# Long convolution beside a feed-forward block: the second transforms of the convolution as 64x32 tiles in plain float32 after a butterfly, with one four-bank buffer

## The chip, the core and the metric

The kernel runs on one core of a Trainium2 chip. The metric is the device time of one execution in microseconds (us), lower is better. TensorE (PE in the profile) does the matrix products, VectorE (DVE) and ScalarE (ACT) the elementwise work, GpSimd (POOL) and SyncE (SP) issue most of the transfers. Matrix products land in PSUM, eight banks of 128 partitions by 512 float32 numbers; everything else on the chip lives in SBUF.

## The reference

The input is `x` (2048 positions, 576 channels). It is normalized, and the output is the sum of the input and two branches:

```python
xn = layernorm(x)
return x + A(xn) + B(xn)
# A: K[d, l] = Re sum_n C[d,n] * exp(dt[d] * A[d,n] * l) * dt[d] * B[d,n], l = 0..2047
#    y = irfft(rfft(xn padded to 4096) * rfft(K padded to 4096))[:2048] + xn * Dskip
# B: silu(xn @ w1) @ w2, w1 is 576 x 4608, w2 is 4608 x 576
```

Branch B is the bulk of the arithmetic. Branch A is a causal convolution along the positions, one filter of 2048 taps per channel.

## The kernel before, in words

**Number format.** The large products are in the format that the code calls F32R. A float32 operand is split into a rounded high part and a remainder, and a product is made of three matrix products (high by high, high by low, low by high) that add up in PSUM. The small products of the tile form 64x32 or 128x32 are in plain float32; the profile shows two records for each of them.

**The feed-forward part** (`ffn`, `up` and `down`) works in blocks: half of the positions, 4 tiles of 128 hidden features, a group of 512 positions. `up` makes one 128x512 tile of the hidden layer (lines L331 to L333), which ACT passes through SiLU and rounds (`gf`, `gh`, L339 and L340) and DVE splits (`gl`, L342). `down` makes one 128x288 half of an output tile with 12 products (L357, PSUM tile `po`), and DVE adds it to the sum in SBUF (`acc`, L361).

**The convolution** is a transform of length 2048 in two steps. Positions are split in 32 by 64 and frequencies likewise. The first step, over 32 positions, is done for the input by `spread` (L161, L162, result in `d1u` in DRAM) and for the filter by `kgen` (which builds the filter in tables; products `kp` at L696 and `z` at L711; result in `d1k`, stored by L724). Then `Dskip` is added to the first rows of `d1k` by a transfer that accumulates (L727).

**The second step** is `spectral`, the place of the change. For each of 32 outer frequencies k it loads 128 rows of `d1u` and of `d1k` (real and imaginary part of 64 positions) on the SP queue, splits both in high and low (`split_of`, L812 on ACT and L813 on DVE), and multiplies each with the 128x128 matrix of that frequency, three products for each half of the channels (`mm3`, L826; PSUM tiles `pk` for the filter, `pu` for the input). ACT copies the spectrum of the filter out in four pieces (`ka`, `kb`, L750 to L753), DVE multiplies the two spectra (L756 to L759) out of PSUM, the product is split, and a second matrix takes it back (`pb`, L826, three products for each half). ACT copies that out (`yo`, L778), and POOL stores it in `d2` (L779). Later `conv_load` and `add_conv` do the last step over 32 frequencies as 16 products in 64x32 tiles of plain float32 (`py`, L847), eight times in the last 80 us.

**PSUM.** `ps1` has two banks (`ph`), `ps2` three (`po`), `pss` three (everything of the convolution).

**The order of the work.** The convolution is a side stream. `weave` advances it between the steps of the feed-forward part: each `yield` of the side stream names the share of the steps at which it goes on. `marks` in `side` gives the shares at which the filter's tables begin, the second step begins and ends: 0.13, 0.597 and 0.823; `tail_at` those of the last step. A scheduler then makes a fixed order for each engine, by priorities (`high_priority`) and by `issue_after` (called through `behind`), which keeps an instruction behind a named one of the same engine. Each engine and each queue executes its order strictly one after the other.

Of the kernel before, what the change touches and what calls it, by code (L numbers as in the profile page):

```python
# [43 lines left out]
def kernel(  # L44
# [15 lines left out]
    cf1: bass.AP,  # L60
    cm23: bass.AP,
    cs4: bass.AP,
    cv: bass.AP,
    out: bass.AP,
):
# [22 lines left out]

    cst = ctx.enter_context(tc.tile_pool(name="cst", bufs=1))
    ident = cst.tile([P, P], F32, name="ident")  # L90
    f1 = cst.tile([P, P], F32, name="f1")
    s4 = None
    vt = cst.tile([P, 69], F32, name="vt")
# [18 lines left out]
    acc = {}  # L112

    def new_xt(blk):
        xh = xtp.tile([P, NKT, 512], F32R, tag="xh", name=f"xh_{blk}")
# [141 lines left out]
    def ffn():  # L257
# [63 lines left out]
        def up(blk, t, a=0, e=512, after=None):  # L321

            half, c, b = blk
            xh, xl, x4 = xts[2 * half + b]
            h1, l1 = W1[half, c, t]
            pool, tag = (ps2, "ps2") if e == 256 and t > 1 else (ps1, "ps1")
            ph = pool.tile([P, 512], F32, tag=tag, name="ph")[:, a:e]
            for n, (w, v) in enumerate(((h1, xh), (h1, xl), (l1, xh))):
                for kt in range(NKT):
                    with behind(after):  # L330
                        nc.tensor.matmul(ph, w[:, kt, :], v[:, kt, a:e], start=n + kt == 0, stop=False)  # L331
            nc.tensor.matmul(ph, h1[:, 4, :], x4[:, a:e], start=False, stop=False)  # L332
            pins["pe"] = nc.tensor.matmul(ph, l1[:, 4, :], x4[:, a:e], start=False, stop=True).ins  # L333
            gf = gp.tile([P, 512], F32, tag="gf", name="gf", bufs=2)[:, a:e]
            if a == 0:
                G[blk, t] = [gp.tile([P, 512], F32R, tag=n, name=n) for n in ("gh", "gl")]
            gh, gl = (g[:, a:e] for g in G[blk, t])
            with tc.high_priority():
                nc.scalar.activation(gf, ph, AF.Silu)  # L339
                pins["gh"] = nc.scalar.copy(gh, gf).ins  # L340
                with behind(pins["w1l2"] if e == 256 else None):
                    pins["gl"] = nc.vector.tensor_sub(gl, gf, gh).ins  # L342

        def down(blk, jj):
# [5 lines left out]
                    add_conv(j, (acc[j], acc[j + 1]))  # L350
            for h in range(2):
                hs = slice(h * HD, (h + 1) * HD)
                po = ps2.tile([P, 512], F32, tag="ps2", name="po")
                n = 0
                for t in range(FT):
                    for g, w in ((0, 0), (0, 1), (1, 0)):
# [227 lines left out]
    def kgen():  # L584
        fT, phiT = kf["f"], kf["phi"]
        with tc.tile_pool(name="kg", bufs=1) as kg:
# [59 lines left out]
            for i in range(NCK):  # L646
# [72 lines left out]
                    nc.scalar.copy(sv[:, h], z[h].rearrange("p (e k c) -> p e k c", e=4, c=2))  # L719
                if r == NRUN - 2:  # L720
                    d0 = (i // NRUN) * NRUN * CH
                    kv = d1k.rearrange("(k n) (g d) -> g n k d", n=64, g=2)
                    for gp_ in range(2):
                        nc.sync.dma_start(kv[gp_, :, :, d0:d0 + NRUN * CH], stage[gp_ * 64:(gp_ + 1) * 64])  # L724
                yield (i + 1) / NCK

        nc.gpsimd.dma_start(d1k.rearrange("(k n) d -> n k d", n=P)[0],  # L727
                            dskip.unsqueeze(0).broadcast_to([32, D]), accum_op=ALU.add)

    def spectral():  # L730
        def operands(k):
            rows = slice(k * P, (k + 1) * P)
            return load_part(d1u[rows, :], "u"), load_part(d1k[rows, :], "k")

        def front(k):
            if k % 2 == 0:
                mm = kl.tile([P, 2, 4, P], F32R, tag="mm", name="mm")
                nc.gpsimd.dma_start(mm, cm23[:, k:k + 2])
                mats.append(mm)
            mk = mats[-1][:, k % 2]  # L740
            us, ks = ops.pop(k) if k in ops else (split_of(t, n) for t, n in zip(operands(k), "uk"))
            ka = kl.tile([P, D], F32, tag="ka", name="ka")
            kb = kl.tile([P, D], F32, tag="kb", name="kb", bufs=1)
            y = kl.tile([P, D], F32, tag="y", name="y", bufs=1)
            y2 = kl.tile([P, D], F32, tag="y2", name="y2", bufs=1)
            for h in range(2):
                hs = slice(h * HD, (h + 1) * HD)
                pk = pss.tile([P, 512], F32, tag="pss", name="pk")
                mm3(pk[:, :HD], [(mk[:, 0], mk[:, 1], ks)], hs)
                nc.scalar.copy(ka[:64, hs], pk[:64, :HD])  # L750
                nc.scalar.copy(ka[64:, hs], pk[:64, :HD])
                nc.scalar.mul(kb[:64, hs], pk[64:, :HD], -1.0)
                nc.scalar.copy(kb[64:, hs], pk[64:, :HD])  # L753
                pu = pss.tile([P, 512], F32, tag="pss", name="pu2")
                mm3(pu[:, :HD], [(mk[:, 0], mk[:, 1], us)], hs)
                nc.vector.tensor_mul(y[:, hs], pu[:, :HD], ka[:, hs])  # L756
                nc.vector.tensor_mul(y2[:64, hs], pu[64:, :HD], kb[:64, hs])
                nc.vector.tensor_mul(y2[64:, hs], pu[:64, :HD], kb[64:, hs])
            nc.vector.tensor_add(y, y, y2)  # L759
            return mk, split_of(y, "y")  # L760

        mats = []
        first = operands(0)
        yield 1.1
        with behind(pins["gh"]):
            ops = {0: [split_of(t, n) for t, n in zip(first, "uk")]}
        yield 1.12
        nxt = front(0)
        for k in range(32):
            mk, ys = nxt  # L770
            if k < 31:
                nxt = front(k + 1)
            yo = kl.tile([P, D], F32, tag="yo", name="yo")
            for h in range(2):
                hs = slice(h * HD, (h + 1) * HD)
                pb = pss.tile([P, 512], F32, tag="pss", name="pb")
                mm3(pb[:, :HD], [(mk[:, 2], mk[:, 3], ys)], hs)
                nc.scalar.copy(yo[:, hs], pb[:, :HD])  # L778
            nc.gpsimd.dma_start(d2.rearrange("(p k) d -> k p d", k=32)[k], yo)  # L779
            yield 1 + (k + 1) / 32  # L780


    order = iter((0, 1, 2, 3, 8, 9, 10, 11, 4, 5, 6, 7, 12, 13, 14, 15))
# [22 lines left out]

    yss = {}

    def split_of(t, tag):
        h = kl.tile([P, D], F32R, tag=tag + "h", name=tag + "h")  # L810
        l = kl.tile([P, D], F32R, tag=tag + "l", name=tag + "l")
        nc.scalar.copy(h, t)  # L812
        nc.vector.tensor_sub(l, t, h)  # L813
        return h, l

    def load_part(rows, tag):
        t = kl.tile([P, D], F32, tag=tag + "r", name=tag + "r")
        nc.sync.dma_start(t, rows)
        return t

    def mm3(dst, terms, hs):

        n = 0
# [13 lines left out]

    def add_conv(j, dsts):

        py = [pool.tile([P, 512], F32, tag=t, name="py") for pool, t in ((pss, "pss"),) * 3 + ((ps2, "ps2"),)]  # L840
# [20 lines left out]
        return (FT + i * 2 * FT + 1) / (2 * NCH * 2 * 2 * FT)  # L861

    def side():
        nonlocal s4, kl, yp, pa, tail_at
        marks = (0.13, 0.597, 0.823)
        tail_at = (0.91, 0.934, 0.967, 0.0072)
        with tc.tile_pool(name="kf", bufs=1) as kfp:
            for n in ("f", "phi"):
                kf[n] = kfp.tile([P, D], F32, name=n + "T")
            with tc.tile_pool(name="par", bufs=1) as par:  # L870
                with tc.tile_pool(name="pa", bufs=4) as pa:

# [54 lines left out]
        s4 = s4p.tile([P, 32], F32, name="s4")  # L927
        nc.gpsimd.dma_start(s4, cs4)

        with tc.tile_pool(name="kl", bufs=2) as kl:  # L930
            for at in spectral():
                yield marks[1] + (at - 1) * (marks[2] - marks[1])
        yp = ctx.enter_context(tc.tile_pool(name="yp", bufs=3))
        yield from tail()

    sd = side()
# [20 lines left out]
def _constants():  # L957
# [5 lines left out]
    s1 = np.zeros((2, 2, 32, 32, 2, 2), f8)  # L963
    f1 = np.zeros((2, 2, 32, 32, 2, 2), f8)
    for q in range(2):
        s1[:, q, :, :, :, q] = cs
# [8 lines left out]
    m2 = np.zeros((32, 2, 64, 2, 64), f8)  # L975
    m2[:, 0, :, 0, :] = c
    m2[:, 1, :, 0, :] = -s
    m2[:, 0, :, 1, :] = s
    m2[:, 1, :, 1, :] = c
# [6 lines left out]
    m3 = m3.reshape(32, P, 4, 16, 2).transpose(0, 1, 3, 2, 4)  # L986
    m23 = np.stack([m2.reshape(32, P, P), m3.reshape(32, P, P)], 1).transpose(2, 0, 1, 3)
    m23 = np.stack([*_hi_lo(m23[:, :, 0]), *_hi_lo(m23[:, :, 1])], 2)
    v = np.concatenate([-64 * np.arange(32.0) - 32, np.arange(33.0), [256, 64, 8, 1]])
    v = np.broadcast_to(v, (P, 69))  # L990
    r = {
# [2 lines left out]
        "cf1": f1,  # L994
        "cm23": m23,
        "cs4": s4,
        "cv": v,
    }
    return {k: np.ascontiguousarray(a, dtype=np.float32) for k, a in r.items()}
# [23 lines left out]
```

## Time and profile before

| What | Before |
| --- | --- |
| time, median of 3 runs | 1110.47 us (1110.06 to 1110.9) |
| span of the profiled execution, first to last instruction | 1108.2 us |
| PE busy | 1102.2 us (99% of the span) |
| DVE busy | 916.6 us (83%) |
| ACT busy | 706.9 us (64%) |
| POOL busy | 72.1 us (7%) |
| transfers, over the span | 148.56 MB, 134 GB/s |

The page gives a span for the profiled execution, and no other time of it. The timed runs are 2.3 us longer than that span, which is what lies around the first and the last instruction. Busy time counts an engine as busy while any of its instructions is under way. Products on PE overlap, so a 128x288 product has a duration of 295 ns while the next one starts 132 ns after it; the distance between two starts is the time that counts. The chain that ended last goes back from the last instruction to what released it, and tells which engine's work set the time.

### The profile page before, as it was taken

What the parts mean: (1) busy time and instruction counts of PE and PEld (TensorE: products, weight loads), DVE (VectorE), ACT (ScalarE), POOL (GpSimd) and SP (SyncE); (2) the same over time, 40 slices, a digit from 0 to 9 for tenths busy, and PEclk for the clock granted to TensorE, in tenths of its full rate; (3) what the DMA queues carried; (4) which work ended last, traced back from release to release, by engine and by line L of the source; (5) the groups of instructions that cost most, each with busy time, mean ns of one, the idle gap of its engine ahead of it and who ended that gap; (6) DMA issues with size and microseconds to landing.
All of it is one profiled execution on the core that took longest, in us unless ns stands there. A gap on an engine that the chain in (4) does not pass through costs nothing.

```text
span 1108.2 us, 22917 instructions
## 1 busy us (share of the span) xinstructions
PE 1102.2 (99%) x9167; PEld 997.5 (90%) x9167; DVE 916.6 (83%) x1543; ACT 706.9 (64%) x1222; POOL 72.1 (7%) x129
## 2 busy tenths in 40 slices
PE   9999999999999999999999999999999999999998
PEld 7989998899998899899999989999999999999887
DVE  7799899999999999999999737787778778784433
ACT  4564466676677676677867536877777878774210
POOL 1100000000000000011000000000000000000111
PEclk9999999999999999999999999999999999999999
DMA  9745512525252525264744173554544455434983
GB/s 270 190 123 160 152 50 61 120 73 131 77 121 83 116 72 118 77 174 154 206 122 103 45 179 109 162 167 123 156 145 152 138 149 170 129 107 127 241 224 87
DMA packets 175755, 148.56 MB, mean 134 GB/s; under 512 B 111088, under 2 KB 142592, under 8 KB 175520
## 3 DMA queue, kind: packets, MB, share of 16 engines
q1 hardware_dynamic: 165328, 112.63, 38.7%
q0 software_dynamic: 9568, 33.62, 9.6%
q8 instruction: 72, 1.18, 0.5%
q10 hardware_dynamic: 752, 0.85, 0.3%
q14 instruction: 35, 0.29, 0.1%
HBM read 102.53 MB, written 44.61 MB: 133 GB/s over the span
## 4 chain that ended last, share of the span: by engine, by line
PE 98%; DMA 1%; DVE 1%; SPq 0%; issue 0%; DVEq 0%
PE po L357 42%; PE ph L331 35%; PE kp L696 3%; PE ph L332 3%; PE ph L333 3%; PE pu L826 2%; PE pb L826 2%; PE pk L826 2%; PE z L711 2%; PE pu L161 1%; PE py L847 1%; DMA acc<-in_A_u_dram 1%; PE pu L162 1%; PE pt L124 0%; DVE w1l L295 0%; PE ptk L490 0%
## 5 line engine op out<-in xcount | busy, mean ns | idle before, releaser
L357 PE MATMUL po<-w2l,gh 128*128 128x288 f32 x1152 | 338.5, 295 | 0.0
L357 PE MATMUL po<-w2h,gl 128*128 128x288 f32 x1152 | 336.4, 295 | 0.0
L357 PE MATMUL po<-w2h,gh 128*128 128x288 f32 x1152 | 336.1, 295 | 0.0
L357 PEld LDWEIGHTS po<-w2h,gh 128*128 128x128 f32 x1152 | 215.2, 188 | 7.7 <-issue 2.8
L357 PEld LDWEIGHTS po<-w2l,gh 128*128 128x128 f32 x1152 | 215.9, 188 | 5.1 <-issue 0.5
L357 PEld LDWEIGHTS po<-w2h,gl 128*128 128x128 f32 x1152 | 215.4, 188 | 0.9
L339 ACT ACTIVATE gf<-ph 128x512 f32<-128x512 f32 (+1 forms) x148 | 86.4, 584 | 143.8 <-PE ph L333 134.8
L331 PE MATMUL ph<-xh,w1l 128*128 128x512 f32 (+1 forms) x592 | 161.3, 385 | 0.0
L331 PE MATMUL ph<-xh,w1h 128*128 128x512 f32 (+1 forms) x592 | 161.3, 387 | 0.0
L331 PE MATMUL ph<-xl,w1h 128*128 128x512 f32 (+1 forms) x592 | 161.1, 385 | 0.0
L361 DVE TENSOR_TENSOR acc<-po,acc 128x288 f32<-128x288 f32 x288 | 126.2, 451 | 37.0 <-PE po L357 35.6
L342 DVE TENSOR_TENSOR gl<-gf,gh 128x512 fp32r<-128x512 f32 (+1 forms) x148 | 99.0, 672 | 64.6 <-ACT gh L340 63.8
L331 PEld LDWEIGHTS ph<-xh,w1l 128*128 128x128 f32 x592 | 108.0, 188 | 20.0
L331 PEld LDWEIGHTS ph<-xl,w1h 128*128 128x128 f32 x592 | 107.9, 188 | 19.8
L331 PEld LDWEIGHTS ph<-xh,w1h 128*128 128x128 f32 x592 | 104.5, 188 | 16.7 <-ACT x L133 0.5
L340 ACT CAST gh<-gf 128x512 fp32r<-128x512 f32 (+1 forms) x148 | 89.5, 608 | 9.5 <-PE po L357 6.6
L653 ACT ACTIVATE c<-th,magic 128x1040 f32<-128x1040 f32 x36 | 42.1, 1168 | 37.9 <-DVE C L676 28.0
L655 ACT ACTIVATE c<-th 128x1040 f32<-128x1040 f32 x36 | 38.7, 1075 | 33.6 <-DVE th L654 33.6
L314 ACT CAST w2h<-w2r 128x576 fp32r<-128x576 f32 x72 | 47.0, 671 | 17.7 <-PE po L357 14.9
L295 DVE TENSOR_TENSOR w1l<-w1r,w1h 128x640 fp32r<-128x640 f32 x72 | 56.9, 817 | 0.2
L332 PE MATMUL ph<-x,w1h 128*128 128x512 f32 (+1 forms) x148 | 57.0, 386 | 0.0
L333 PE MATMUL ph<-x,w1l 128*128 128x512 f32 (+1 forms) x148 | 56.9, 385 | 0.0
(185 smaller groups left out, 1828.8 us busy)
## 6 DMA issues: line engine op xcount, KB each, us to landing
w2r<-in_B_w_dram SPq DMA_DIRECT2D x72, 288.0 KB, 3.8
w1r<-in_B_w_dram SPq DMA_DIRECT2D x35, 512.0 KB, 3.8
d1u<-u POOLq DMA_DIRECT2D x32, 288.0 KB, 2.5
d1k<-stage SPq DMA_DIRECT2D x18, 512.0 KB, 6.8
ur<-d1u SPq DMA_DIRECT2D x32, 288.0 KB, 3.7
kr<-d1k SPq DMA_DIRECT2D x32, 288.0 KB, 2.9
d<-yo POOLq DMA_DIRECT2D x32, 288.0 KB, 4.0
ys<-d SPq DMA_DIRECT2D x32, 288.0 KB, 11.8
```

Of the source, the lines that this page charges most:

```text
L295: pins["w1l"] = nc.vector.tensor_sub(l1, src, h1).ins
L314: pins["w2h"] = nc.scalar.copy(h2, r2).ins
L331: nc.tensor.matmul(ph, w[:, kt, :], v[:, kt, a:e], start=n + kt == 0, stop=False)
L332: nc.tensor.matmul(ph, h1[:, 4, :], x4[:, a:e], start=False, stop=False)
L333: pins["pe"] = nc.tensor.matmul(ph, l1[:, 4, :], x4[:, a:e], start=False, stop=True).ins
L339: nc.scalar.activation(gf, ph, AF.Silu)
L340: pins["gh"] = nc.scalar.copy(gh, gf).ins
L342: pins["gl"] = nc.vector.tensor_sub(gl, gf, gh).ins
L357: pins["pe"] = nc.tensor.matmul(po[:, :HD], G[blk, t][g][:, js], W2[half, c, t][w][:, hs], start=n == 0, stop=n == 3 * FT - 1).ins
L361: nc.vector.tensor_add(acc[j][:, hs], po[:, :HD], acc[j][:, hs])
L653: nc.scalar.activation(c65, th, AF.Identity, bias=magic)
L826: nc.tensor.matmul(dst, st, mv[:, hs], start=n == 0, stop=n == 3 * len(terms) - 1)
```

## The change

The second step works on pairs of outer frequencies, p = 0 to 15, and the 64 positions of the second step are split in two halves. With the sum and the difference of the halves (the butterfly) the even and the odd frequencies come apart, and each needs half of the matrix.

- For the input, the butterfly is put in the constants of the first step: `s1` now writes the two combinations to `d1u`. For the filter, DVE does it in `halves`, three operations on 128x576 for each pair, after `load_k` has fetched the rows (the second half twice, once with the two groups of 32 partitions exchanged).
- `visit` replaces the three F32R products of 128x128: 16 products of 64x32 tiles in plain float32 for each pair, for the filter (`response`) and for the input (`inputs`). They come in the order half h, row group g, column group o, with o innermost.
- The split of `u` and `k` in high and low goes. The spectrum of the product is still split, and the way back (`back`) still takes 12 F32R products for each pair.
- PSUM: `pss` (three banks) and a new `ps3` (one bank) exist outside of the stage; within it they give way to `psb`, one buffer of four banks. Each visit and each `back` fills it and ACT empties it with two copies of 128x576 (`clear`), so that it is used 48 times in turn. DVE multiplies from SBUF. `ps2` has two banks instead of three; outside of the stage `ps3` takes every third `po`.
- All loads of the stage go on the POOL queue, and `d1k` is stored in four transfers of 32 partitions instead of two of 64.
- The stage ends at 0.86 of the steps instead of 0.823. `f1` and `vt` live in a pool that is freed before the stage.

The core of the diff:

```diff
-    ps2 = ctx.enter_context(tc.tile_pool(name="ps2", bufs=3, space=PSUM))
-    pss = ctx.enter_context(tc.tile_pool(name="pss", bufs=3, space=PSUM))
+    ps2 = ctx.enter_context(tc.tile_pool(name="ps2", bufs=2, space=PSUM))
+    pss = psb = ps3 = None
...
-                mm3(pk[:, :HD], [(mk[:, 0], mk[:, 1], ks)], hs)
-                nc.scalar.copy(ka[:64, hs], pk[:64, :HD])
-                nc.scalar.copy(ka[64:, hs], pk[:64, :HD])
-                nc.scalar.mul(kb[:64, hs], pk[64:, :HD], -1.0)
-                nc.scalar.copy(kb[64:, hs], pk[64:, :HD])
...
-                mm3(pu[:, :HD], [(mk[:, 0], mk[:, 1], us)], hs)
-                nc.vector.tensor_mul(y[:, hs], pu[:, :HD], ka[:, hs])
-                nc.vector.tensor_mul(y2[:64, hs], pu[64:, :HD], kb[:64, hs])
-                nc.vector.tensor_mul(y2[64:, hs], pu[:64, :HD], kb[64:, hs])
...
+        def halves(p):
+            if p > 15:
+                return
+            t, w = ks[p]
+            c = cwt[:, p]
+            nc.vector.scalar_tensor_tensor(w[:, 0], w[:, 1], c[:, 0:1], w[:, 0], op0=ALU.mult, op1=ALU.add)
+            for m in range(2):
+                nc.vector.scalar_tensor_tensor(t[:, m], w[:, 0], c[:, 1 + m:2 + m], t[:, 1], op0=ALU.mult, op1=ALU.add)
+
+        def visit(p, t, name):
+
+            banks = psb.tile([P, 2, 2, 512], F32, tag="psb", name=name)
+            last = pins["pe"]
+            for n, (h, g) in enumerate(((0, 1), (0, 0), (1, 1), (1, 0))):
+                gs = slice(64 * g, 64 * g + 64)
+                for o in range(4):
+                    os = slice(32 * o, 32 * o + 32)
+                    with tc.high_priority(), behind(last):
+                        last = nc.tensor.matmul(banks[os, g, h, :HD], mats[p, 0][gs, os], t[gs, o % 2, h * HD:(h + 1) * HD],
+                                                start=True, stop=True, tile_position=(64 * g, 32 * o),
+                                                skip_group_check=True).ins
+            pins["pe"] = last
+            return banks
+
+        def response(p):
+
+            kas = [kl.tile([P, D], F32, tag="ka", name="ka") for _ in range(2)]
+            clear(visit(p, ks.pop(p)[0], "pk"), kas)
+            for g in range(2):
+                ka, kb = kas[g], kl.tile([P, D], F32, tag="kb", name="kb")
+                nc.scalar.mul(kb[:64], ka[64:], -1.0)
+                nc.scalar.copy(kb[64:], ka[64:])
+                nc.scalar.copy(ka[64:], ka[:64])
+                kab[2 * p + g] = ka, kb
+
+        def clear(banks, dsts):
+
+            with tc.high_priority():
+                for g in range(2):
+                    nc.scalar.copy(dsts[g].rearrange("p (h d) -> p h d", h=2), banks[:, g, :, :HD])
...
+        for p in range(16):
+            if p < 15:
+                response(p + 1)
+                load_m(p + 1, 1)
+            load_k(p + 3)
+            yield 1.1 + 0.9 * (3 * p + 1) / 48
+            halves(p + 2)
+            if p < 15:
+                inputs(p + 1)
+            load_u2(p + 2)
+            yield 1.1 + 0.9 * (3 * p + 2) / 48
+            back(p)
+            load_m(p + 2, 0)
+            yield 1.1 + 0.9 * (3 * p + 3) / 48
...
-        marks = (0.13, 0.597, 0.823)
+        marks = (0.13, 0.597, 0.86)
```

`load_k` issues six transfers for a pair, `load_u` one, `load_m` one for each of two matrices, and `back` stores two tiles of `yo`, all on the POOL queue. `inputs` does for each half of the pair two multiplications of half height, one of full height, an addition and the split, all on 128x576 or 64x576.

More of the change, by code (lines that the diff above doesn't have):

```diff
@@ L108, with banks_of @@
     ps1 = ctx.enter_context(tc.tile_pool(name="ps1", bufs=2, space=PSUM))
-    ps2 = ctx.enter_context(tc.tile_pool(name="ps2", bufs=3, space=PSUM))
-    pss = ctx.enter_context(tc.tile_pool(name="pss", bufs=3, space=PSUM))
+    ps2 = ctx.enter_context(tc.tile_pool(name="ps2", bufs=2, space=PSUM))
+    pss = psb = ps3 = None
     acc = {}
+    def banks_of():
+        n = 0
+        while True:
+            n += 1
+            pool, tag = (ps3, "ps3") if ps3 and n % 3 == 0 else (ps2, "ps2")
+            yield pool.tile([P, 512], F32, tag=tag, name="po")
+    spare = banks_of()
     def new_xt(blk):
@@ L721, in kgen @@
                     d0 = (i // NRUN) * NRUN * CH
-                    kv = d1k.rearrange("(k n) (g d) -> g n k d", n=64, g=2)
+                    kv = d1k.rearrange("(h k n) (g d) -> g h n k d", h=2, n=32, g=2)
                     for gp_ in range(2):
-                        nc.sync.dma_start(kv[gp_, :, :, d0:d0 + NRUN * CH], stage[gp_ * 64:(gp_ + 1) * 64])
+                        for h in range(2):
+                            o = gp_ * 64 + h * 32
+                            nc.sync.dma_start(kv[gp_, h, :, :, d0:d0 + NRUN * CH], stage[o:o + 32])
@@ L762, in spectral @@
-        mats = []
-        first = operands(0)
-        yield 1.1
[L765 to L780, printed above, removed]
+        uv = d1u.rearrange("(m p r) d -> p r m d", m=2, r=P)
@@ new lines, in spectral, with load_u, load_k @@
+        kv = d1k.rearrange("(m p r) d -> p m r d", m=2, r=P)
+        cwt = kl.tile([P, 16, 3], F32, name="cwt", bufs=1)
+        nc.sync.dma_start(cwt, cw)
+        us, ks, mats, kab, ys = {}, {}, {}, {}, {}
+        def load_u(p):
+            t = kl.tile([P, 2, D], F32, tag="u", name="u")
+            nc.gpsimd.dma_start(t, uv[p])
+            us[p] = t
+        def load_k(p):
+            if p > 15:
+                return
+            t = kl.tile([P, 2, D], F32, tag="k", name="k")
+            w = kl.tile([P, 2, D], F32, tag="kw", name="kw", bufs=1)
+            nc.gpsimd.dma_start(t[:, 1], kv[p, 0])
+            nc.gpsimd.dma_start(w[:, 0], kv[p, 1])
+            for r in range(4):
+                nc.gpsimd.dma_start(w[32 * r:32 * r + 32, 1], kv[p, 1, 32 * (r ^ 1):32 * (r ^ 1) + 32])
+            ks[p] = t, w
@@ new lines, in inputs @@
+        def inputs(p):
+            uts = [kl.tile([P, D], F32, tag="ut", name="ut") for _ in range(2)]
+            clear(visit(p, us.pop(p), "pu2"), uts)
+            for g in range(2):
+                ka, kb = kab.pop(2 * p + g)
+                y = kl.tile([P, D], F32, tag="y", name="y", bufs=1)
+                y2 = kl.tile([P, D], F32, tag="y2", name="y2", bufs=1)
+                nc.vector.tensor_mul(y, uts[g], ka)
+                nc.vector.tensor_mul(y2[:64], uts[g][64:], kb[:64])
+                nc.vector.tensor_mul(y2[64:], uts[g][:64], kb[64:])
+                nc.vector.tensor_add(y, y, y2)
+                ys[2 * p + g] = [kl.tile([P, D], F32R, tag=n, name=n, bufs=2) for n in ("yh", "yl")]
+                yh, yl = ys[2 * p + g]
+                nc.scalar.copy(yh, y)
+                nc.vector.tensor_sub(yl, y, yh)
@@ new lines, in back @@
+        def back(p):
+            pb = psb.tile([P, 2, 2, 512], F32, tag="psb", name="pb")
+            last = pins["pe"]
+            for g in range(2):
+                mk = mats[p, 1][:, g]
+                parts = ys.pop(2 * p + g)
+                for h in range(2):
+                    hs = slice(h * HD, (h + 1) * HD)
+                    for n, (w, v) in enumerate(((0, 0), (0, 1), (1, 0))):
+                        with tc.high_priority(), behind(last):
+                            last = nc.tensor.matmul(pb[:, g, h, :HD], mk[:, w], parts[v][:, hs], start=n == 0, stop=n == 2).ins
+            pins["pe"] = last
+            yos = [kl.tile([P, D], F32, tag="yo", name="yo") for _ in range(2)]
+            clear(pb, yos)
+            for g in range(2):
+                nc.gpsimd.dma_start(d2.rearrange("(p k) d -> k p d", k=32)[2 * p + g], yos[g])
@@ new lines, in load_u2 @@
+        def load_u2(p):
+            if p < 16:
+                load_u(p)
+        load_k(0)
+        load_m(0, 0)
+        load_u(0)
+        yield 1.0
+        with behind(pins["gh"]):
+            halves(0)
+        load_m(0, 1)
+        load_m(1, 0)
+        yield 1.03
+        load_k(1)
+        load_u(1)
+        yield 1.05
+        response(0)
+        yield 1.07
+        halves(1)
+        yield 1.085
+        inputs(0)
+        load_k(2)
+        yield 1.1
+        for p in range(16):
[12 more added lines that the diff above has]
+            yield 1.1 + 0.9 * (3 * p + 3) / 48
```

98 lines of the change are left out of this document (48 added, 50 removed).

## The prediction

> **What bounds the kernel now.** I read the busy times and the slices of the page first, then the chain that ended last, and then the stage itself.
>
> ```profile
> span 1108.2 us, 22917 instructions
> PE 1102.2 (99%) x9167; PEld 997.5 (90%) x9167; DVE 916.6 (83%) x1543; ACT 706.9 (64%) x1222; POOL 72.1 (7%) x129
> PE   9999999999999999999999999999999999999998
> PEclk9999999999999999999999999999999999999999
> PE 98%; DMA 1%; DVE 1%; SPq 0%; issue 0%; DVEq 0%
> ```
>
> PE is busy from end to end at the full granted clock, and the chain is PE for 98%: no other engine is waited for, apart from the first transfer. So a product that goes shortens the run by its distance to the next start, as long as nothing else becomes late. The stage in question:
>
> ```profile
> 665.00:985.00 320.00, 320.00 (x2018) 297.24 (x2017) 252.46 (x460) 244.38 (x509) 22.62 (x42) 1.00 0.48 144
> L826 PE MATMUL pk<-kh,mm x128: 288/294/304, 674.7 to 997.3; 128*128 128x288 f32 x128
> L826 PE MATMUL pk<-kl,mm x64: 293/295/298, 675.5 to 997.2; 128*128 128x288 f32 x64
> L826 PE MATMUL pu<-uh,mm x128: 290/294/302, 674.8 to 1002.1; 128*128 128x288 f32 x128
> L826 PE MATMUL pu<-ul,mm x64: 292/294/298, 674.9 to 1002.0; 128*128 128x288 f32 x64
> ```
>
> The first line is the busy time in one stretch of 320 us (in order: PE, weight loads, DVE, ACT, POOL, granted clock, share of the transfer engines, GB/s). PE never idles in it; DVE is at 79%, ACT at 76%. The other four are the products that the change replaces, 128 + 64 + 128 + 64 = 384.
>
> **The products that go.** The timeline of PE around one set:
>
> ```profile
> 703.76 0.29 PE L826 MATMUL pk<-kh,mm 128*128 128x288 f32 x1
> 703.89 0.30 PE L826 MATMUL pk<-kl,mm 128*128 128x288 f32 x1
> ...
> 704.82 0.29 PE L826 MATMUL pk<-kh,mm 128*128 128x288 f32 x1
> 704.95 0.62 PE L331 MATMUL ph<-xh,w1h 128*128 128x512 f32 x2
> ```
>
> Nine products take 704.95 - 703.76 = 1.19 us, 0.132 us each. 384 x 0.132 = 50.8 us leave PE. The 192 products of the way back stay as they are.
>
> **The visits that come.** A visit is 16 products of 64x32 tiles in float32 with 288 columns. The kernel has just that form in `add_conv`, so its price is a row (each product has two records, hence x32):
>
> ```profile
> 1031.45 0.39 PE L332 MATMUL ph<-x,w1h 128*128 128x512 f32 x1
> 1031.68 0.39 PE L333 MATMUL ph<-x,w1l 128*128 128x512 f32 x1
> 1032.00 1.23 PE L847 MATMUL py<-ys,s 64*32 64x288 f32 x32
> 1033.16 0.40 PE L357 MATMUL po<-w2h,gh 128*128 128x288 f32 x1
> 1033.40 0.29 PE L357 MATMUL po<-w2l,gh 128*128 128x288 f32 x1
> 1059.88 0.39 PE L333 MATMUL ph<-x,w1l 128*128 128x512 f32 x1
> 1060.20 1.31 PE L847 MATMUL py<-ys,s 64*32 64x288 f32 x32
> 1061.44 0.40 PE L357 MATMUL po<-w2h,gh 128*128 128x288 f32 x1
> 1061.68 0.29 PE L357 MATMUL po<-w2l,gh 128*128 128x288 f32 x1
> ```
>
> In the first block the 512-wide product at 1031.68 would be followed after 0.23 us (the distance before it), at 1031.91; the tiles begin at 1032.00, so going in costs 0.09. The block takes 1033.16 - 1032.00 = 1.16. The first 288-wide product after it takes 0.24 to the next start in place of 0.13, so coming out costs 0.11. Together 1.36 us. The second block gives 0.09 + 1.24 + 0.11 = 1.44. I take 1.36, since nothing in a visit waits in between; the ends are 1.16 (no cost of going in and out) and 1.44. 32 x 1.36 = 43.5 us. The built order of the changed kernel sets each visit as one run among the feed-forward products, except the first: one product, five feed-forward products, then fifteen. That is one more going in and out (0.20) and one half-filled round (half of 1.16), 0.8 us. In the last 80 us that order has the products of `add_conv` in seven runs where there were eight, 0.2 us less. PE's sum: -50.8 + 43.5 + 0.8 - 0.2 = -6.7 us; with the ends of a visit, -13.1 and -4.1.
>
> The Trainium skill (TensorE: Matmul & The Clock Gate, Part 3, The mechanism) says that a weight load overlaps with products in flight only when the row group differs. In `add_conv` the row group alternates from product to product; a visit keeps it for four products. By that rule the four would go one after another and the sum would not be -6.7 but that of the last rival below. The rows of `kp` quoted there speak against it.
>
> **DVE and ACT.** Per pair of frequencies DVE had 8 operations of 576 columns and 12 of 288, and now has 13 of 576. ACT had 6 of 576 and 20 of 288, and now has 14 of 576.
>
> ```profile
> L759 DVE TENSOR_TENSOR y<-y,y 128x576 f32<-128x576 f32 x32 | 24.0, 751 | 0.0
> L756 DVE TENSOR_TENSOR y<-pu,ka 128x288 f32<-128x288 f32 x64 | 29.0, 453 | 14.3 <-ACT ka L751 13.3 <-PE pu L826 0.2
> L812 ACT CAST yh<-y 128x576 fp32r<-128x576 f32 x32 | 21.6, 674 | 29.1 <-DVE y L759 29.0
> L361 DVE TENSOR_TENSOR acc<-po,acc 128x288 f32<-128x288 f32 x288 | 126.2, 451 | 37.0 <-PE po L357 35.6
> ```
>
> DVE: 8 x 0.75 + 12 x 0.45 = 11.4 us before, 13 x 0.75 = 9.8 after. ACT: 6 x 0.67 + 20 x 0.40 = 12.0 before (0.40 from the pieces of `pk`), 14 x 0.67 = 9.4 after. And the stage is 16% longer (0.263 of the steps for 0.226). Both engines get lighter, all of it beside PE: nothing in the sum.
>
> **One buffer for the stage.** Each of 48 uses waits until ACT has emptied the one before, two copies, 2 x 0.67 = 1.35 us. PE is in order, so all feed-forward products stand behind a use that waits. In the built order the shortest distance between two uses is 27 feed-forward products, 24 x 0.132 + 3 x 0.23 = 3.9 us, so ACT may begin 2.5 us late. Counting ACT's order beside PE's, the worst place is the first clearing of an input: ten ACT instructions stand ahead of it, it ends 2 us before PE comes to the next use; elsewhere 2.5 us or more are left. I take zero. With that cover gone, every microsecond is 48.
>
> **Two banks for `po`.** A group of 12 products, 1.59 us, now covers one addition (0.45 us) and what DVE does before it; in the built order that is one or two operations of 0.75, and other products often stand between two groups. I take zero. The late thing would be `acc`, and behind it the next group of PE. Some 80 groups lie in the stage: 0.1 us each would be 8 us.
>
> **The queues.** Eleven transfers per pair go to POOL, 176 in all, 0.54 us each (row of `d` below): about 6 us of each 18 us, off the path. The load of `k` stands behind the two stores of `yo`, which wait for the clearing, but its visit is 15 us later. SP loses 64 loads and stores `d1k` in 36 transfers instead of 18, with the same bytes. Zero, while POOL keeps up.
>
> **The start of the stage.** Here the data are tight.
>
> ```profile
> 642.16 1.16 PE L711 MATMUL z<-f,kt 64*128 64x128 f32 x16
> 643.25 1.20 PE L331 MATMUL ph<-xh,w1h 128*128 128x512 f32 x4
> 644.53 3.56 SPq L724 DMA_DIRECT2D d1k<-stage  x2
> 653.05 0.86 POOL L727 DMA_DIRECT2D d1k<-in_A_Dskip_dram  x1 [27.31 <-DMA d1k<-stage]
> 657.76 0.32 SPq L818 DMA_DIRECT2D kr<-d1k  x1
> kr<-d1k SPq DMA_DIRECT2D x32, 288.0 KB, 2.9
> d<-yo POOLq DMA_DIRECT2D x32, 288.0 KB, 4.0
> L779 POOL DMA_DIRECT2D d<-yo x32 | 17.3, 541 | 204.5 <-ACT yo L778 204.4
> ```
>
> The last `z` ends at 643.25, `d1k` has landed at 653.05, `Dskip` by 657.76. After the change POOL issues the five loads of the second half right behind `Dskip` (653.9 to 656.6, landed by about 660.6 with the 4.0 of the row) and the first half four transfers later, at about 659.5, landed 2.9 to 4.0 later, 662.4 to 663.5. Two operations of DVE follow, so the filter is ready at 664 to 665. The built order has 24.5 us of feed-forward products between the last `z` and the first visit: 667.7. Some 3 us are left, and I take zero. If the four stores of `d1k` or the loads take 4 to 7 us longer than that, PE stands still for 1 to 4 us, once. No row shows a gain here.
>
> **Sum.** -6.7 us. The profiled execution goes from 1108.2 to 1101.5; the median of the runs stands 2.27 above that span, so 1110.47 - 6.7 = 1103.8 us.
>
> **Rivals.**
>
> 1. Late start. As above, 1 to 4 us once: 1105 to 1108. For it: a chain of three transfers. Against: 3 us in hand.
> 2. The other side: the single buffer holds PE up. It needs ACT to begin a clearing over 2.5 us after the visit. It takes back the gain at 6.7 / 48 = 0.14 us per use and makes the run slower by over 0.2% (2.2 us) from (6.7 + 2.2) / 48 = 0.19 us per use; at 0.5 us per use 1128. For it: ACT at 76% in the stage before. Against: less work on it, and 2 us left at the worst place.
> 3. Additions of DVE come late for two banks: 0.1 us for each of 80 groups, 1112.
> 4. It doesn't shorten PE at all: 50.8 / 32 = 1.59 us per visit, where going in and out would cost 0.43 instead of 0.20: 1110.5. No block of `py` is that dear.
> 5. The row groups. This is what the rule of the Trainium skill named above would do here:
>
> ```profile
> L696 PE MATMUL kp<-C 128*32 128x64 f32 x1152 | 35.2, 222 | 0.0
> ```
>
> A block of 16 has four waves of 0.29 us (1.16 / 4), eight tiles in each. If the four column groups of one row group had to follow each other, a visit would be 4 x 1.16 + 0.20 = 4.84 us, and the run 1110.5 - 50.8 + 32 x 4.84 = 1215 us. For it: no row has four products of one row group of 64 in a run. Against: `kp` uses all 128 rows and only the column group changes, and 1152 x 0.222 = 256 us of products lie in 35.2 us of busy time, seven in flight.
>
> **How the numbers follow.** Forecast (1101.5 to 1105) 0.62; late start 0.17; single buffer 0.09; two banks 0.05; no shortening 0.05; row groups 0.02. 0.2% is 2.2 us, about what a measurement can tell from no change: below 1108.25 is faster. Forecast and late start are faster but for 0.01 of the latter, and a little of the single buffer is too: 0.80. Within 0.2% lie no shortening and parts of the two banks and the single buffer: 0.08. Slower 0.12. The range goes from 1100.5 (a visit of 1.26, between 1.16 and 1.36) to 1108.5, the end of the late start; it leaves out the other rivals.
>
> **What would show it.** Right: 32 runs of 64x32 tiles, each 1.3 to 1.45 us from the last start before it to the normal distance after it; PE without idle time; `clear` following its visit at once and ending before the next use. Wrong: idle time of PE in front of a visit or a `back` with ACT as its end (the buffer), in front of `po` with DVE (the banks), in front of the first visit with a transfer or `halves` (the start); visits near 5 us (row groups).

## The result and the profile after

The changed kernel takes 1117.31 us (median, 1115.56 to 1118.75), against 1110.47 before: 1.0059 times as long, 95% interval 1.0047 to 1.0071. It is slower by 6.8 us where the prediction had it faster by 6.7, and it lies outside the predicted range. The profiled execution took 1118.75 us, the slowest of those timed, with a span of 1116.9 us, 8.7 more than before. The profiled execution before was a little faster than its median: the results that give both list a time 1.8 to 1.9 us above the span of the same execution, not 2.3, so 1108.2 goes with about 1110.05. The terms below therefore add up to about 1.9 us more than the medians show.

The page after, with the lines that answer to those shown of before (busy times, slices of 27.9 us, the chain):

```profile
span 1116.9 us, 23956 instructions
...
PE 1097.8 (98%) x9807; PEld 962.2 (86%) x9807; DVE 892.1 (80%) x1431; ACT 660.7 (59%) x1030; POOL 141.8 (13%) x257
...
PE   9999999999999999999999999999999999996998
...
PEclk9999999999999999999999999999999999998999
...
PE 8%; DMA 4%; SPq 0%; DVE 0%; ACT 0%; issue 0%
PE po L367 4%; DMA w2r<-in_B_w_dram 3%; PE ph L341 2%; DMA ys<-d 1%; PE py L944 1%; DMA d<-yo 0%; PE ph L343 0%; PE ph L342 0%; ACT w2h L324 0%; SPq L315 0%; SPq L292 0%; SPq L932 0%; SPq L291 0%; SPq L288 0%; DVE acc L371 0%
```

Three things differ. PE is busy for less time than before (1097.8 for 1102.2), so work did leave it. One slice near the end has PE at 6 and the clock at 8. And the chain has new names in it: it can be followed back only a short way (its shares add up to 12%), and in that stretch stand the loads of `w2r`, the loads of `ys` and the queue of SP, where before it was PE alone.

The stage, in the same stretch of 320 us as before:

```profile
665.00:985.00 320.00, 317.39 (x2697) 265.39 (x2696) 236.91 (x365) 208.07 (x341) 88.30 (x163) 1.00 0.51 156
```

PE idles for 2.6 us of it (before: none). DVE is busy for 236.9 us instead of 252.5, ACT for 208.1 instead of 244.4. The timeline of PE around one visit, one that nothing delays:

```profile
676.33 1.20 PE L795 MATMUL pu<-u,m 64*32 64x288 f32 x32
677.46 1.20 PE L341 MATMUL ph<-xh,w1l 128*128 128x512 f32 x4
```

The block takes 677.46 - 676.33 = 1.13 us. Where nothing waits, the block with going in (0.09 to 0.10) and coming out (0.10 to 0.11) is 1.33 us in the mean; 32 of them and 0.8 for the split first visit are 43.3 us. The predicted price was 1.36 each and 44.3 together. The visits are not where the time went.

What PE waited for from 640 to 1035 us (total, times, longest), and the end of the largest wait:

```profile
PE po L367 <- ACT w2h L324: 9.9, 3, 8.6
PE po L367 <- DVE gl L352: 0.8, 1, 0.8
PE po L367 <- DVE w2l L326: 0.4, 1, 0.4
```

```profile
1010.47 0.61 PE L341 MATMUL ph<-xh,w1h 128*128 128x512 f32 x2
1019.73 1.09 PE L367 MATMUL po<-w2h,gh 128*128 128x288 f32 x3 [8.65 <-ACT w2h L324]
1020.62 1.05 PE L341 MATMUL ph<-xh,w1h 128*128 128x512 f32 x2
1021.47 0.44 PE L367 MATMUL po<-w2l,gh 128*128 128x288 f32 x1
1021.71 0.44 PE L367 MATMUL po<-w2h,gl 128*128 128x288 f32 x1
...
1022.76 1.09 PE L341 MATMUL ph<-xl,w1h 128*128 128x512 f32 x4
```

PE stands for 8.65 us, 40 us after the stage is over (its last product starts at 971.3). Behind the wait the products are 0.24 us apart (1021.47, 1021.71) where they otherwise are 0.13 apart; that ends at 1022.6: the clock has dropped, which costs another 1.4 us. ACT, which PE waited for, waited itself:

```profile
1019.01 0.67 ACT L324 CAST w2h<-w2r 128x576 fp32r<-128x576 f32 x1 [12.79 <-DMA w2r<-in_B_w_dram]
```

and the queue of SP shows why the load was late (start, time on the queue, instruction):

```profile
976.19 0.38 SPq L288 DMA_DIRECT2D w1r<-in_B_w_dram  x1
...
977.82 1.06 SPq L315 DMA_DIRECT2D w2r<-in_B_w_dram  x2
978.92 2.55 SPq L932 DMA_DIRECT2D ys<-d  x2
...
992.72 13.40 SPq L932 DMA_DIRECT2D ys<-d  x10
1006.63 1.58 SPq L900 DMA_DIRECT2D r<-dr  x2
1009.10 11.73 SPq L315 DMA_DIRECT2D w2r<-in_B_w_dram  x3
```

The same queue before the change:

```profile
991.42 11.50 SPq L305 DMA_DIRECT2D w2r<-in_B_w_dram  x3
1013.35 0.38 SPq L278 DMA_DIRECT2D w1r<-in_B_w_dram  x1
...
1014.97 1.06 SPq L305 DMA_DIRECT2D w2r<-in_B_w_dram  x2
1016.07 1.28 SPq L835 DMA_DIRECT2D ys<-d  x2
```

Before, the last weights went out in the order in which they were needed: three of `w2r`, which wait for free buffers, from 991.42; then the last five loads, whose tiles lie in a pool that takes the memory of the stage, once the stage was over; then `ys`. After, the stage is over some 38 us earlier (its last product starts at 971.3; before, at 1009.6). The last five loads can go at once, `ys` is pinned behind the load that was written last in the program, which is one of these five, and so 16 loads of `ys` of 288 KB and four of `r` of 576 KB enter the queue ahead of the three of `w2r`. SP needs 13.40 us for ten of them. The first of the three weights is issued at 1009.10, and its data land 9.9 us later, just before ACT starts at 1019.01.

My theory was from here on: the order on SP's queue makes the tail stall, and without it the change is worth its visits. Against it stood two others: that the traffic of `ys` delays any weight at that time, whatever its queue, and that the stage simply ends too early, so that its mark is the cause.

### The profile page after: what moved, and what is told of

Its sections match the earlier page's. It is cut to its first block, busy times and chain, and to the rows that moved or that the text cites. A ratio compares the mean times of both kernels' runs of the same rounds, so it can differ in the third digit from the quotient of the medians.

```text
span 1116.9 us, 23956 instructions
## 1 busy us (share of the span) xinstructions
PE 1097.8 (98%) x9807; PEld 962.2 (86%) x9807; DVE 892.1 (80%) x1431; ACT 660.7 (59%) x1030; POOL 141.8 (13%) x257
## 5 line engine op out<-in xcount | busy, mean ns | idle before, releaser
L367 PE MATMUL po<-w2h,gh 128*128 128x288 f32 x1152 | 338.6, 298 | 10.2 <-ACT w2h L324 10.1
L341 PE MATMUL ph<-xl,w1h 128*128 128x512 f32 (+1 forms) x584 | 158.7, 387 | 0.0
L174 POOL DMA_DIRECT2D d1u<-u x32 | 17.4, 545 | 463.5 <-ACT u L173 463.5
L326 DVE TENSOR_TENSOR w2l<-w2r,w2h 128x576 fp32r<-128x576 f32 x72 | 53.2, 750 | 18.7 <-ACT w2h L324 18.5
L832 ACT CAST yh<-y 128x576 fp32r<-128x576 f32 x32 | 21.6, 674 | 65.1 <-DVE y L829 53.2
```

The costliest lines, as they stand in the source:

```text
L174: nc.gpsimd.dma_start(d1u.rearrange("(p m j) d -> m j p d", m=2, j=NJ)[m, j], u1)
L326: pins["w2l"] = nc.vector.tensor_sub(l2, r2, h2).ins
L367: pins["pe"] = nc.tensor.matmul(po[:, :HD], G[blk, t][g][:, js], W2[half, c, t][w][:, hs], start=n == 0, stop=n == 3 * FT - 1).ins
L832: nc.scalar.copy(yh, y)
```

## The experiments

**The weights' loads put ahead of `ys`.** Only the pin changes: `ys` now stands behind the last of the loads in the order of need.

```diff
             pins["load"] = nc.sync.dma_start(r2, w2v[:, c * FT + t, :]).ins
+            if last and t == 1:
+                pins["w2s"] = pins["load"]
...
-        with behind(pins["load"]):
+        with behind(pins["w2s"]):
```

> The changed kernel, and the first loads of the last step (ys, r0) are kept behind the weight load w2r of the last chunk's second tile instead of behind the load that is traced last; in the built order all weights then stand ahead of the 16 loads of ys on the SP queue. Queue theory (the ys loads stand ahead of urgent weights on SP, and PE waits for these): the 8.8 us of idle PE at 1011 us and the 1.4 us of half clock behind it are gone, 1117.3 - 10.2 = 1107 us, and the visits stay at 1.33 us. Bandwidth theory (the transfers are too many at that time, in whatever order): PE still waits 4 us or more there, 1111 us or more. Stage theory (the single buffer and two banks are what costs): no change, 1116 to 1118 us.

Measured: 1107.67 us (1107.31 to 1108.63), ratio to before 0.9977 (0.9968 to 0.9986), span 1105.9. SP's queue, and a stretch of 10 us (the last three numbers of the row are the granted clock, the share of the transfer engines and GB/s):

```profile
995.20 4.63 SPq L315 DMA_DIRECT2D w2r<-in_B_w_dram  x3
999.88 1.27 SPq L934 DMA_DIRECT2D ys<-d  x2
...
1006.23 12.18 SPq L934 DMA_DIRECT2D ys<-d  x10
```

```profile
1010.00:1020.00 10.00, 10.00 (x71) 9.62 (x70) 2.29 (x5) 0.94 (x2) 0.00 (x0) 1.00 1.08 258
```

The three weights go out at 995.20, 13.9 us earlier, the long load of `ys` comes behind them, and PE no longer stops between 960 and 1035 us, not even beside a share of 1.08. Between the medians 9.6 us come back. But this edit also makes `ys` later and changes the order of PE, DVE and ACT from 998 us on, so order and traffic are not told apart by it.

**The same pin in the kernel before.** The same two edits there.

> The kernel before the change with only the same loads put ahead. If the order of the queue matters only because the shorter stage lets the loads of ys go early, it gives nothing here, where every weight was issued before the first ys: 1109.5 to 1111 us. If the pin itself was worth something to any version, it becomes faster by 1 us or more, and the 2.6 us by which the pinned changed kernel beats the one before are not the butterfly's.

Measured: 1110.93 us, ratio 0.9999 (0.999 to 1.0007). The pin gives nothing by itself; what the pinned changed kernel gains on the kernel before, 0.23%, comes from the rest of the change.

**Only the three weights moved to another queue.** The changed kernel, `ys` as early as in it and the order of PE, DVE and ACT the same; the three loads leave SP.

```diff
-            pins["load"] = nc.sync.dma_start(r2, w2v[:, c * FT + t, :]).ins
+            if half == 1 and (c == NCH - 1 and t < 2 or c == NCH - 2 and t > 2):
+                nc.gpsimd.dma_start(r2, w2v[:, c * FT + t, :])
+            else:
+                pins["load"] = nc.sync.dma_start(r2, w2v[:, c * FT + t, :]).ins
```

> The changed kernel as it is, with only the three last loads of second weights (those that stood behind the 16 loads of ys on SP) moved to the POOL queue; every engine's order is otherwise the same, and ys starts as early as before. If these three are late because they stand behind ys in SP's order, they are issued as soon as a buffer comes free (about 985 to 998 us), the 8.7 us of idle time at 1010 us and the slower clock behind it go, and the run takes 1107 to 1109 us. If it is the traffic of ys that makes any weight late at that time, whatever its queue, they land 10 us or more after their issue, PE still stands for 4 us or more between 995 and 1020 us, and the run stays at 1113 us or above.

Measured: 1108.3 us (1107.72 to 1110.3), ratio 0.9982 (0.9973 to 0.9991). The three issues on POOL, and the transfer engines in the same time:

```profile
996.87 0.54 POOL L316 DMA_DIRECT2D w2r<-in_B_w_dram  x1 [22.52 <-DMA ys<-d]
999.68 0.54 POOL L316 DMA_DIRECT2D w2r<-in_B_w_dram  x1 [2.26 <-DMA ys<-d]
1008.52 0.54 POOL L316 DMA_DIRECT2D w2r<-in_B_w_dram  x1 [8.30 <-DVE w2l L329]
```

```profile
990.00:1000.00 10.00, 10.00 (x66) 9.31 (x65) 3.89 (x8) 2.47 (x4) 0.86 (x2) 1.00 1.09 257
1000.00:1010.00 10.00, 10.00 (x57) 8.85 (x56) 2.52 (x4) 3.01 (x5) 0.76 (x2) 1.00 1.07 250
```

The profile puts POOL's first two waits down to loads of `ys`; what frees the buffers are the splits of the weights before, which end at 996.58, 999.39 and 1008.23 us, 0.29 us ahead of each issue. The engines are as full as in the changed kernel (1.09 and 1.08 there), and the weights are slow: 8.1 to 8.6 us from issue to landing for the three and 12.0 for one that stayed on SP, where the median of all `w2r` in the changed kernel is 4.1. But the first of the three is issued 12.2 us earlier than there, and PE never stops from 960 to 1035 us. So the order is the cause: the traffic makes a load 4 to 8 us slower, which the loads have in hand; the place in the queue costs 12 us, which they have not. The traffic has a part in that price: SP needs 13 us for ten loads of `ys` beside full engines, where the first two took 1.28 us before the change.

**`ys` on the POOL queue.** The reverse: `ys` leaves SP, the weights stay.

```diff
-                nc.sync.dma_start(yss[j][64 * h:64 * h + 64],
+                nc.gpsimd.dma_start(yss[j][64 * h:64 * h + 64],
```

> The changed kernel, and the loads of ys go to the POOL queue instead of SP, at the same point of the program; r0 stays on SP. So the weights are no longer behind them in a queue, but the same bytes are under way at the same time. Queue theory: 1107 us, the w2r load that came at 1009 us is issued by about 990. Bandwidth theory: it is issued early and lands late all the same (8 us or more after its issue), PE waits 4 us or more, 1111 us or more. Stage theory: 1116 to 1118 us.

Measured: 1122.84 us (1122.24 to 1123.83), ratio 1.0114 (1.01 to 1.0128), slower than the changed kernel: the theory of the queue had 1107 us and missed. In the tail PE stands 12.4 us for ACT, and ACT waits for a weight (the wait of ACT from 985 us on, then SP's queue):

```profile
ACT w2h L324 <- DMA w2r<-in_B_w_dram: 17.8, 1, 17.8
```

```profile
978.37 3.16 SPq L900 DMA_DIRECT2D r<-dr  x4
...
984.00 11.42 SPq L291 DMA_DIRECT2D w1r<-in_B_w_dram  x1
995.51 2.58 SPq L315 DMA_DIRECT2D w2r<-in_B_w_dram  x1
...
1001.26 21.25 SPq L315 DMA_DIRECT2D w2r<-in_B_w_dram  x3
```

With two queues issuing, the four loads of `r` and ten of `ys` are out by 985 us, and then SP needs 11.42 us for one transfer of 64 KB. The weight that ACT waits for is the one behind it: issued at 995.51, where the changed kernel has 985.53, and landed 16.9 us later, where it is 12.3 there. So here the traffic itself does harm, as the theory of the traffic says: 10 us by holding SP, and some 5 us more on the way. That the order is the cause holds for the changed kernel, where the run before this one shows it, and not for every way to spread the same loads. The Trainium skill (DMA: Bandwidth & Descriptors, Issuing engines are not separate DMA queues) says that transfers of all issuing engines end on the same 16 engines, so that another queue saves only the time to issue. In this run the engines are as full on two queues as on one (a share of 1.05 from 990 to 1000 us, against 1.09 in the changed kernel) and move 262 GB/s instead of 243, so the second queue adds little. Why the one transfer took 11.42 us where the same transfer at 987 us in the run above took 0.5 is not settled; more bytes had been issued by then, but no run changed that alone.

**The end of the stage moved.** Two runs of the changed kernel, with its last mark at 0.89 and at 0.823, the value of before, in place of 0.86.

> The changed kernel with the end of the stage at 0.89 of the steps instead of 0.86, nothing else. In the built order the urgent w2r load then stands behind 4 of the 16 loads of ys instead of behind all of them. Queue theory: the wait of PE near the tail falls from 8.8 us to 3 us or less, 1107 to 1111 us. Bandwidth theory: the burst comes 30 us later and meets the last chunk's weights, the wait stays or moves, 1113 us or more. Stage theory: the stage is 11% longer, so its own waits of 3.6 us shrink by 1 or 2, 1115 us.

> The changed kernel with the end of the stage at 0.823 of the steps, as in the kernel before: that part of the change undone. In the built order the ys loads come some 40 us earlier, mixed with the weights of the second but last chunk; the w2r load that was late still stands behind all of them, but they have been issued by about 970 us. Queue theory: the wait at 1011 us is gone, another of 0 to 8 us may stand some 40 us ahead of it, 1107 to 1115 us. Stage theory: the denser stage has more waits of its own than 3.6 us, 1118 us or more.

Measured: at 0.89 1110.13 us (1106.88 to 1113.44), ratio 0.9996 (0.9983 to 1.001). The wait in the tail shrinks from 8.65 to 2.8 us, since two of the three weights now go out ahead of most of `ys`; but the clock still drops behind it (a mean of 0.83 from 1010 to 1020 us), and PE waits 3.2 us for DVE and ACT elsewhere (first kernel below), so a part is lost again. The profiled execution took 1112.47 us, above the median. At 0.823 1127.66 us, ratio 1.0157 (1.0143 to 1.017), where the theory of the stage had 1118 us or more and that of the queue 1107 to 1115. The wait in the tail is gone, as the latter said: PE doesn't stop from 985 to 1035 us. But PE stands 12.6 us between 940 and 985 us, and the granted clock is 0.66 and 0.50 in the two stretches of 10 us from 950 to 970. What PE waited for, from 640 us on at 0.89 and from 940 to 985 us at 0.823:

```profile
PE po L367 <- ACT w2h L324: 2.8, 1, 2.8
PE po L367 <- DVE acc L371: 1.8, 3, 1.2
...
```

```profile
PE pb L846 <- ACT ut L816: 4.0, 1, 4.0
...
PE pb L846 <- ACT yo L816: 1.4, 1, 1.4
PE pu L795 <- ACT ka L816: 1.4, 1, 1.4
```

At 0.823 a wait stands in front of a `back` (`pb`) and a visit (`pu`) with ACT's clearing (`ut`, `yo`, `ka`) as its end. That is the single buffer, the prediction's second rival: in the changed kernel it costs nothing, and here, among its last uses in a stage that is packed closer, it does. So the mark decides whether and where `ys` meets the weights, but at the mark of 0.86 a change of the order alone removes the tail's loss (the first and third run above). An earlier end makes new waits; a later one puts two of the three weights ahead and pays for it with waits elsewhere.

**Each visit twice.** The pinned kernel, with the same 16 products done a second time into the same places; the rest of the computation is as it was.

```diff
-            for n, (h, g) in enumerate(((0, 1), (0, 0), (1, 1), (1, 0))):
+            for n, (h, g) in enumerate(((0, 1), (0, 0), (1, 1), (1, 0)) * 2):
```

> The kernel with the weights' loads put ahead, and in it each visit's 16 products done twice (the same products into the same places, so nothing is left out). If the price of a visit is right and all of it lies on PE's path, the second pass adds the block alone (1.13 to 1.16 us, no second going in and out) for each of 32 visits: 36 to 37 us, so 1143 to 1146 us after 1107.7. If the visits had cover (PE idle beside them anyway), clearly less, under 1135. If a longer hold of the one buffer delays the clearing and the next use, more: 1150 and above, with idle time of PE in front of visits that ACT ends.

Measured: 1138.61 us, ratio 1.0249 (1.0235 to 1.0263), span 1137.3, which is 31.4 more than that of the pinned kernel.

```profile
676.79 2.17 PE L797 MATMUL pu<-u,m 64*32 64x288 f32 x64
678.89 1.19 PE L343 MATMUL ph<-xh,w1l 128*128 128x512 f32 x4
```

The double block takes 2.10 us, so the second 16 products add 0.97, and 32 x 0.97 = 31.0 us against the 31.4 of the span: all of a visit lies on PE's path. That the two agree to 0.4 us is in part luck: a wait of 1.67 us at 688 us with 3.4 us of half clock behind it is new in this run, and the waits of the pinned kernel at 713 and 747 us are gone, which comes out nearly even. I had expected 1.13 to 1.16 for the second half, and so 1143 to 1146 us; the number was wrong because a block by itself contains 0.16 us that doesn't grow with its length.

**A third buffer for `w2r`.** Meant for the 2.6 us of idle time within the stage.

```diff
-... tag="w2r", name="w2r", bufs=2)
+... tag="w2r", name="w2r", bufs=2 if last and t > 1 else 3)
```

> The kernel with the weights' loads put ahead, and three buffers instead of two for the raw second weights. If the 3.5 us that PE still idles in the stage (683, 713, 747, 755 us) come from weights loaded too late because a buffer of two comes free late, the idle time at 747 us goes and 1 to 3 us with it: 1105 to 1106.7 us. If these stalls come from DVE being late with the splits (the load is early enough), nothing changes: 1107.2 to 1108.2 us, with the same idle time at the same places.

Measured: 1109.53 us (1107.08 to 1111.6), ratio 0.9987 (0.9978 to 0.9996): outside of both theories' bounds. The wait at 747 us is gone, but the buffer changed the order of every engine, the stage starts 2.6 us later (its first product at 671.0 instead of 668.4), and other waits came (one of 2.16 us at 707 us, with a granted clock of 0.93 and 0.90 from 700 to 720):

```profile
PE po L369 <- DVE acc L373: 2.6, 2, 2.2
```

So this run doesn't tell the two theories apart. It does show additions of DVE coming late, the third rival. The cause of the 2.6 us in the changed kernel can be read from its timeline (DVE, SP, ACT and PE in turn) at the largest of its places:

```profile
744.22 1.42 DVE L326 TENSOR_TENSOR w2l<-w2r,w2h 128x576 fp32r<-128x576 f32 x2
...
745.00 4.83 SPq L315 DMA_DIRECT2D w2r<-in_B_w_dram  x3
...
748.02 0.67 ACT L324 CAST w2h<-w2r 128x576 fp32r<-128x576 f32 x1 [2.48 <-DMA w2r<-in_B_w_dram]
...
748.74 0.40 PE L367 MATMUL po<-w2h,gh 128*128 128x288 f32 x1 [1.11 <-ACT w2h L324]
```

DVE comes to the split of the weights at 744.22, a buffer comes free and SP issues the next load at 745.00, it lands for ACT at 748.02, and PE starts at 748.74. ACT stood idle for 2.48 us there: it is the order in which DVE takes its work that makes the load late, then the load that holds ACT and PE. That is a reading of one trace; no run removed it alone.

## Why the prediction was wrong

- **The visits** (1.36 us, 44.3 together): right, 1.33 and 43.3. The first visit is split as said. Each visit is wholly on PE's path, by the doubled visits.
- **Rival 5, the row groups**: refuted. Four products of one row group follow one another in every visit, and its block takes 1.13 us, as short as the alternating block of `py` (1.16) and a quarter of the 4.64 that the rule would give. In the trace of the visit at 676.33 us the four products of one row group start within 0.05 us of each other, each after its own weight load, and the next four 0.27 us after the first. The rule of the Trainium skill (TensorE: Matmul & The Clock Gate, Part 3, The mechanism), by which a weight load overlaps only where the row group differs, does not hold for these tiles. **Rival 4**, no shortening, falls with the same number.
- **The start of the stage**: right. The first visit starts at 668.71 (667.7 was said), without a wait. **Rival 1** did not happen.
- **One buffer for the stage, two banks for `po`**: zero was right in the changed kernel to 0.3 us: none of its waits has a clearing at its end, and only the smallest in the stage (0.13 us, at 756 us) an addition. The cover is thin, though: the mark at 0.823 brings out the first, the third `w2r` buffer and the mark at 0.89 the second.
- **DVE and ACT** ("beside PE: nothing in the sum"): their work fell as said, but the waits did not stay at zero. At 683, 713, 747 and 756 us the starts of PE are 0.89 (in two parts), 0.99, 1.27 and 0.29 us further apart than the products need, 3.4 us in all. The step looked at how much work the two have and not at the order in which they come to the splits of the feed-forward part: weights at 683 and 747 us, a hidden tile at 713. This cost nearly half of the gain. Why the two are late was read at 747 us only.
- **The queues** ("SP loses 64 loads ... Zero, while POOL keeps up"): this is the step that failed. It counted what leaves and enters each queue in the stage and did not ask what an earlier end of the stage lets go earlier. The loads of `ys` stand behind a load that waits for the stage's memory; the stage's end moved from 1009.6 to 971.3, and with it `ys` moved ahead of three weights that wait for buffers. The built order showed just that. The price: the 8.65 us wait (8.8 between starts) and 1.4 of half clock, 10.2 us.

The sum with these terms: PE's own part is -50.8 + 43.3 - 0.2 = -7.7, and -7.7 + 3.4 + 10.2 = +5.9 us; the span shows +8.7. Of the other 2.8, 0.8 lie ahead of the stage (the last run of `z` starts at 642.93 instead of 642.16), 1.4 behind the first `py` (1.2 more than before, where 0.2 less was predicted) and 0.6 between. Behind the first `py`, 0.57 us are a wait of a `py` for an addition (`r`) at 1099 us, which the kernel before doesn't have. The rest was not followed up.

With the failed step repaired the mechanism is worth what is left: the pinned kernel is 2.6 us faster than the one before in the medians, where -7.7 + 3.4 = -4.3 would follow; the difference is within the 2.8 us that were not explained. It has the lowest median of all versions here; the one with three weights on POOL (0.9982) can't be told from it.

## What to carry to other kernels

When a change makes a stage end earlier, list what was waiting for that end: freed memory and pins let transfers go, and on a queue in order they go ahead of all that is behind them. A load that is pinned "behind the last one in the program" is not behind the last one needed, so pin bulk loads behind the one that is needed latest. Read the built order of each queue against the order of need before costing a queue at zero; a busy engine's slack says nothing about the place of a transfer.

## What was not expected of the hardware

- **A wait can cost more than its length.** In the stretch of the long wait the granted clock is 0.79 in the mean (the third number from the end):

```profile
1010.00:1020.00 10.00, 1.35 (x6) 0.84 (x5) 0.29 (x1) 0.99 (x2) 0.00 (x0) 0.79 0.68 206
```

The Trainium skill (TensorE: Matmul & The Clock Gate, Loop structure matters more than you think) says that 8 us of idle PE halve its clock. The trace agrees: after 8.65 us the products are 0.24 us apart instead of 0.13 for 2.9 us. Much shorter waits did the same in other runs: behind 2.77 us (the mark at 0.89), 2.16 us (the third buffer) and 1.67 us (the doubled visits) the clock was at half for 3.4 us, which costs 1.7 us, more than behind the long one. The wait of 1.11 us at 747 us left the clock at 1.00 in its stretch (740 to 750 us).

- **A full set of transfer engines makes each load 2 to 3 times as slow**: 8.1 to 12.0 us from issue to landing for a weight at a share of 1.07 to 1.09, against a median of 4.1; with `ys` on a second queue it was 16.9 for one.
- **A block of 16 tiles has a fixed part**: 1.13 us for 16 products, 2.10 for 32. Longer visits would be cheaper for each product.
